# Local attention and top-2 mixture of experts on one core: attention on quarters of the array, whole loads of tile pairs, routing in phases, row writes spread over two blocks

## The chip, the core and the metric

The kernel runs on one core of one Trainium2 chip. The core has a matrix engine (TensorE, PE in the profile, with PEld for its weight loads), VectorE (DVE), ScalarE (ACT), GpSimd (POOL) and SyncE (SP), and 16 DMA engines that move data between HBM and the on-chip memory. The metric is the device time in microseconds. Before the change it is 1012.22 us, the median of three runs (1010.86 to 1013.97).

## The reference, cut to what matters

Eight batches of 576 positions and eight heads of 64 make 4608 tokens of 512 values. Attention is local: a chunk of 64 positions sees itself only. Then each token goes to the two best of eight experts by noisy logits.

```python
scores = scale * np.matmul(q_c, k_c.transpose(0, 1, 2, 4, 3))       # chunks of 64
attn = softmax(scores); out = np.matmul(attn, v_c)                    # x: 4608 x 512
noisy = x @ w_gate + np.log1p(np.exp(x @ w_noise)) * noise
top2, top2_w = the two largest of noisy, softmax over the two
for e in range(8):
    for k in range(2):
        h = np.maximum(x[mask] @ w1[e], 0.0)                          # 512 -> 1024
        out[mask] += top2_w[mask, k, None] * (h @ w2[e])              # 1024 -> 512
```

## The kernel before

The tokens are cut into 36 tiles of 128 (two chunks of 64, eight heads as four pairs). The order of work on each engine is written out by hand: each engine runs its own list in program order and waits on semaphores.

**Attention.** `attend(it)` is one turn of a software pipeline over tiles. On TensorE it holds the scores of tile it (L390), attention times values of tile it−2 (L416), the transposition of the probabilities of tile it−1 (L406), the transposition of the result x of tile it−3 (L431) and the gate product of tile it−4 (L444). VectorE takes the maximum (L394) and subtracts it (L399), and divides the result by its row sums (L420, L423, L426). ScalarE does the exponential (L402) and copies PSUM out (L408, L435). K and V of a tile lie in a ring of six buffers that are zero off the diagonal, so that one product over 128 rows handles two heads: each half of a tile is loaded by itself (L357, L362), with q (L355) that makes five loads a tile, all issued by SP.

**Routing.** After the gate, groups of tiles, (first tile, count) = (0,4), (4,8), (12,4), (16,4), (20,8), (28,8), are routed by a generator `route(g)` whose steps are spread between VectorE's steps by `step_route(n)`, with idle yields while ScalarE or TensorE work for it. It finds the two experts of each token (L484, L488), and its rank in each expert's list by a product with a triangle of ones (L507, L509), and from these the row of a slot table in HBM. `scatter` on GpSimd then writes 128 rows of x with an indirect DMA (L567) for each tile and each of the two choices; a one-element copy into `spacer` (L565) delays it until the turn has got that far.

**Experts.** Expert 0 has three blocks of rows (three, three and four tiles of 128 slots, the last of 64), computed while the last routing is still on. Block 0 and block 1 are read once the tokens below 16 and below 28 are in the slot table (`EARLY`), block 2 after all. `gather(i)` issues a block's loads on SP (L198, dynamic for later experts L203). `x_tile` transposes the gathered rows (L242 on TensorE for the first blocks, L246 on VectorE for later ones), `layer1` and `layer2` multiply in high and low halves, three products each (`three`, L259), with L278 and L281 between the layers; `weigh` (L288) scales an output by its token's weight and `store` adds it to `out` by an indirect DMA on GpSimd (L226). `out` is zeroed first by 37 writes of 256 KB (`zero_out`, L626). The other experts follow in an order that is found at run time; SP reads it from memory (L772) before it can load their weights (`w_load`, L103 and L105). `w_split` (L116, L117) cuts staged weights into halves.

SP's list after attention, then, is: 28 zero writes, block 1's gather, nine zero writes, block 2's gather, the reads of the order, expert 1's w1 (four loads of 512 KB), the gather of the following block.

Of the kernel before, what the change touches and what calls it, by code (L numbers as in the profile page):

```python
# [19 lines left out]
P = 128  # L20
# [29 lines left out]
def kernel(ctx, tc, qT, kT, vh, wgn, noise, w1, w2, out, caps=CAPS):  # L50
# [36 lines left out]
    nc.vector.memset(caprow[:, 0:1], float(caps[0]))  # L87
    run8 = consts.tile([P, NE], FT, name="run8")
# [32 lines left out]
    gate = pg.enter_context(tc.tile_pool(name="gate", bufs=1, side="right"))  # L121
# [11 lines left out]
    EARLY = {0: 2, 1: 4}  # L133
# [3 lines left out]
    groups = [(0, 4), (4, 8), (12, 4), (16, 4), (20, 8), (28, 8)]  # L137
# [14 lines left out]
    rot = {"xg": 0, "tr": 0, "l1": 0, "l2": 0}  # L152
# [131 lines left out]
    def weigh(i, j, r, p):  # L284
        e = BL[i][0]
        o = OB[0].tile([P, DM], FT, name="o")
        w = weights_of(i, j)[0:r]
        nc.vector.tensor_scalar(o[0:r], p[0:r], w, None, op0=OP.mult)  # L288
# [51 lines left out]
    vs = pv_pools.enter_context(tc.tile_pool(name="vs", bufs=1, side="right"))  # L340
    loads = pk.enter_context(tc.tile_pool(name="loads", bufs=1))
    RING = 6
    KB = [loads.tile([P, 2, 4, P], FT, name=f"kb{n}") for n in range(RING)]
    VB = [vs.tile([P, 2, 2, 4, 65], FT, name=f"vb{n}") for n in range(RING)]
    QB = {}
    HALF = (slice(0, 64), slice(64, 128))
    for n in range(RING):
        for t in (KB[n], VB[n]):
            for h in range(2):
                (nc.vector if n < 2 else nc.gpsimd).memset(t[HALF[1 - h], h], 0.0)  # L350

    def load_qk(t):
        if t < NT:
            QB[t] = loads.tile([P, 4, P], FT, name="qb", bufs=RING)
            nc.sync.dma_start(QB[t], qT[:, t])  # L355
            for h in range(2):
                nc.sync.dma_start(KB[t % RING][HALF[h], h], kT[HALF[h], t])  # L357

    def load_v(t):
        if t < NT:  # L360
            for h in range(2):
                nc.sync.dma_start(VB[t % RING][HALF[h], h], vh[HALF[h], t])  # L362

    nc.scalar.preload_act_table_set("natural_log_exp_and_others")
    for j in range(5):
        load_qk(j)
        if j:
            load_v(j - 1)
# [7 lines left out]

    PR, PT, XS, XT, RC = {}, {}, {}, {}, {}
    by_head = lambda a: a.rearrange("p (g k) -> p g k", k=64)
    sco = [by_head(PS[:, b, :]) for b in range(2)]
# [7 lines left out]
    def scores(t):  # L387
        for hp in range(4):
            for s in HALF:
                nc.tensor.matmul(PS[s, t % 2, hp * P:(hp + 1) * P], QB[t][:, hp, s], KB[t % RING][:, :, hp, s], start=True, stop=True)  # L390

    def soft_max(t):
        mx = work.tile([P, 8], FT, name="mx", bufs=2)
        nc.vector.tensor_reduce(mx, sco[t % 2], AX.X, OP.max)  # L394
        return mx

    def soft_sub(t, mx):
        PR[t] = work.tile([P, 512], FT, name="pr")
        nc.vector.tensor_tensor(by_head(PR[t]), sco[t % 2], mx[:, :, None].to_broadcast([P, 8, 64]), OP.subtract)  # L399
# [12 lines left out]
    def pv(t):  # L412
        for hp in range(4):
            for c, s in enumerate(HALF):
                o = 130 * (hp % 2)
                nc.tensor.matmul(PS[s, 3 + hp // 2, o:o + 130], PT[t][:, hp, s], VB[t % RING][:, :, c, hp, :], start=True, stop=True)  # L416

# [7 lines left out]
    def norm_c(t):  # L425
        nc.vector.tensor_tensor(x_at(t)[:, 0:DM].rearrange("p (b g k) -> p b g k", b=2, k=64), pvb[:, :, :, 0:64], RC[t].to_broadcast([P, 2, 4, 64]), OP.mult)  # L426
# [6 lines left out]
    def x_copy(t):  # L433
        XT[t] = gx.tile([P, ND, P], FT, name="xt")
        nc.scalar.activation(XT[t].rearrange("p d n -> p (d n)"), PS[:, 5, :], AF.Copy)  # L435

    def lg_at(t, n=1):
        g = grp_of[t]
        c = 256 * (g % 2) + 16 * (t - groups[g][0])
        return PS[:, 6, c:c + 16 * n]  # L440

    def gate_mm(t):
        for d in range(ND):
            nc.tensor.matmul(lg_at(t), XT[t][:, d, :], wg[:, d, 0:16], start=(d == 0), stop=(d == ND - 1))  # L444

    IDLE = 6

    def route(g):
# [9 lines left out]
        lg = lg_at(t0, G).rearrange("p (g a e) -> p g a e", a=2, e=NE)  # L458
# [3 lines left out]
        parts = [(XS[t0 // 4 + a], slice(4 * a, 4 * a + 4)) for a in range(G // 4)]  # L462
        nc.scalar.activation(y, lg[:, :, 1, :], AF.Abs)
# [4 lines left out]
        for _ in range(IDLE):  # L468
            yield

        V.scalar_tensor_tensor(u, u, -1.0, y, op0=OP.add, op1=OP.subtract)
        yield
        V.tensor_sub(sp, sp, u)
        yield
        V.scalar_tensor_tensor(sp, z[:, :, 1, :], 0.0, sp, op0=OP.max, op1=OP.add)
        yield
        V.tensor_mul(sp, sp, nz[:, t0:t0 + G, :])
        yield
        V.tensor_add(sp, sp, z[:, :, 0, :])
        yield  # L480
        m = gate.tile(n8, FT, name="gm")
        mi = gate.tile(n8, U32, name="gmi")
        for r in range(G):
            V.max(m[:, r], sp[:, r])  # L484
            if r % 2:
                yield
        for r in range(G):
            V.max_index(mi[:, r], m[:, r], sp[:, r])  # L488
            if r % 2:
                yield  # L490
        oh = gate.tile([P, 2, G, NE], FT, name="goh")
        for k in range(2):
            V.tensor_tensor(oh[:, k], be(e_row), br(mi[:, :, k]), OP.is_equal)
            yield
        for x, s in parts:
            V.scalar_tensor_tensor(x.bitcast(I32)[:, :, CODE], mi[:, s, 0], 8192.0, tok[:, ts][:, s], op0=OP.mult, op1=OP.add)
        ohb = gate.tile([P, G + 1, NE], BF, name="gohb")
        V.memset(ohb[:, G], 0.0)
        V.tensor_add(ohb[:, 0:G], oh[:, 0], oh[:, 1])
        ex, sm = nm("gex"), nm("gsm")  # L500
        V.tensor_sub(ex, m[:, :, 1], m[:, :, 0])
        yield
        nc.scalar.activation(ex, ex, AF.Exp)
        for _ in range(IDLE):
            yield
        rk = PS[:, 7, o:o + 8 * (G + 1)].rearrange("p (g e) -> p g e", e=NE)
# [3 lines left out]
        for _ in range(IDLE):  # L510
            yield
        V.tensor_scalar(sm, ex, 1.0, 1e-9, op0=OP.add, op1=OP.add)
        for i in EARLY:
            if g == EARLY[i] + 1:
                V.tensor_scalar(run8[:, 0:1], run8[:, 0:1], float(NE * P * (blocks[0][i][-1][0] + 1)), None, op0=OP.max)
        yield
        r8 = n3("gr8")
        V.scalar_tensor_tensor(r8, rk[:, 0:G], 8.0, be(run8), op0=OP.mult, op1=OP.add)
        for x, s in parts:
            V.reciprocal(x[:, :, WA], sm[:, s])  # L520
        yield
        ohr = gate.tile([P, 2, G, NE], FT, name="gohr")
        V.tensor_mul(ohr, oh, r8[:, None].to_broadcast([P, 2, G, NE]))
        V.scalar_tensor_tensor(run8, rk[:, G], 8.0, run8, op0=OP.mult, op1=OP.add)
        yield
        for i in EARLY:
            if g == EARLY[i]:
                V.tensor_copy(lim0[i], run8[:, 0:1])
        if g == LAST:

# [7 lines left out]
            yield  # L538
# [9 lines left out]
            yield  # L548
        with nc.allow_low_precision(reason="one whole number below 2**24 among zeros"):
            V.tensor_reduce(lii[:, :, ts], ohr, AX.X, OP.add)  # L550
        for x, s in parts:
            V.tensor_mul(x[:, :, WB], ex[:, s], x[:, :, WA])
        yield
# [50 lines left out]
    def step_route(n):  # L604
        for _ in range(n):
            while routing:
                try:
                    next(routing[0])
                    break
                except StopIteration:  # L610
                    routing.pop(0)

    def finish_route():
        while routing or pending:
            step_route(1)
# [12 lines left out]
    def attend(it):  # L628
        STEPS = 2
        if it > 0:  # L630
            load_qk(it + 4)
            load_v(it + 3)
# [6 lines left out]
        if it in (12, 14, 16, 18):  # L639
            w_load(0, 1, (it - 12) // 2)  # L640
        if it in (29, 31, 33, 35):
            w_load(0, 2, (it - 29) // 2)
        if it < NT:
# [7 lines left out]
        if 0 <= it - 4 < NT:  # L651
            gate_mm(it - 4)
            if grp_of[it - 4] != grp_of.get(it - 3):
                routing.append(route(grp_of[it - 4]))
        if it < NT:
            mx = soft_max(it)
            step_route(STEPS)
            soft_sub(it, mx)
            scatter(1, mx[0:1, 0:1])
            step_route(STEPS)  # L660
            soft_exp(it)
        if 0 <= it - 3 < NT:
            x_copy(it - 3)
        if 0 <= it - 2 < NT:
            norm_a(it - 2)
            step_route(STEPS)
            norm_b(it - 2)
            scatter(1, RC[it - 2][0:1, 0, 0])
            step_route(STEPS)
            norm_c(it - 2)  # L670
            step_route(STEPS)
        if it in range(20, 28):
# [26 lines left out]

    TURNS = (((1, 1), (1, 5), (2, 1)), ((0, 6), (1, 2), (1, 6), (2, 2)))  # L700
    tail = [NT + 2 + a for a in range(2)]

    def hook_tail(f, d):
# [6 lines left out]
        else:  # L710
            step_route(4)

    for i in range(NBL + 1):
# [15 lines left out]
        def hook1(f):  # L729
# [4 lines left out]
            if i == 0:  # L734
                scatter(2, HT[0][f][0][0:1, 0:1].bitcast(FT))
# [8 lines left out]
        def hook2_r(k, f):  # L744
            hook2_f(k, f)
            step_route(2)
            if f % 2 == 0:
# [12 lines left out]
        if i == 0:  # L760
            pa.close()
            block_x(1)
            OB[0] = pb.enter_context(tc.tile_pool(name="ob", bufs=4))
        if i == 0:
            zero_out(NT)
            resolve_early(0)
            layer2(0, hook2_r)
            finish_route()
            last_rows.close()
            block_h(1)  # L770
            for r in range(1, NE):
                place[r] = nc.values_load(order[0:1, r:r + 1], engines=[mybir.EngineType.SP], min_val=0, max_val=NE - 1)  # L772
            for c in range(4):
                w_load(1, 1, c)
# [138 lines left out]
```

## Time and profile before

| quantity | value |
|---|---|
| median of the runs | 1012.22 us |
| profiled execution: time | 1013.9 us |
| profiled execution: span | 1011.6 us |
| mean granted clock of TensorE | 0.989 |
| tile 0's scores, tile 35's scores | 5.5 us, 151.6 us |
| layer 1 and layer 2 of expert 0, block 0, begin | 164.8 us, 189.0 us |
| TensorE busy | 971.4 us (96%) |
| VectorE, ScalarE, GpSimd busy | 453.9 us, 275.8 us, 227.5 us |

The profile shows one execution. A row of the timeline is: start, duration, engine, line, operation, output and inputs by the program's names, the sizes, the number of instructions, and in brackets the idle time in front of it with what ended it. "SPq" is an instruction by which SP issues a DMA.

### The profile page before, as it was taken

The page shows a single profiled execution, that of the slowest core. Times are in us where ns is not written, and L with a number is a line of the kernel's source. Part 1 is how long each engine was busy: PE and PEld are TensorE (multiplying, and loading weights), DVE is VectorE, ACT ScalarE, POOL GpSimd, SP SyncE. Part 2 cuts the span into 40 slices and gives each one's busy share as a digit, 9 for nine tenths or more (in the row PEclk, how much of TensorE's full clock was granted, in tenths as well). Part 3 has the DMA queues.
Part 4 walks back from the last instruction along what each step waited for, and adds up shares of the span by engine and source line. Part 5 has one row for each costly group of instructions (what it writes and reads, how often), then busy time and mean ns, then how long its engine had stood idle before and what let it go on. Part 6 is the DMA issues. An engine that isn't in the chain of part 4 may idle for free. (4 is left out here: it accounts for less than half of the span.)

```text
span 1011.6 us, 16090 instructions
## 1 busy us (share of the span) xinstructions
PE 971.4 (96%) x5930; PEld 874.3 (86%) x5930; DVE 453.9 (45%) x1015; ACT 275.8 (27%) x574; POOL 227.5 (22%) x332
## 2 busy tenths in 40 slices
PE   6999898999799999999999999999999999999996
PEld 5888887898689799989998999899989998999885
DVE  6667665522435354355434542454245334533311
ACT  2444543211314132213211421232123222322200
POOL 3034754751020201110111011101110111101112
PEclk9999999999799999999999999999999999999998
DMA  8899999865470335233622372246235423512213
GB/s 230 260 299 308 339 315 396 308 180 128 81 188 14 64 115 153 32 53 105 172 32 45 112 179 32 42 114 170 32 70 148 105 32 84 167 21 32 32 19 45
DMA packets 103217, 132.92 MB, mean 131 GB/s; under 512 B 22848, under 2 KB 56000, under 8 KB 103136
## 3 DMA queue, kind: packets, MB, share of 16 engines
q1 hardware_dynamic: 86704, 93.54, 30.4%
q0 software_dynamic: 16432, 38.33, 19.2%
q8 instruction: 47, 0.77, 0.3%
q14 instruction: 34, 0.28, 0.1%
HBM read 81.69 MB, written 50.13 MB: 130 GB/s over the span
## 5 line engine op out<-in xcount | busy, mean ns | idle before, releaser
L259 PE MATMUL PS<-xh,w1h 128*128 128x384 f32 (+2 forms) x768 | 262.8, 342 | 9.0 <-DVE hl L281 7.3
L226 POOL DMA_INDIRECT out<-o,lid x77 | 119.3, 1549 | 672.8 <-DVE o L288 645.0
L259 PE MATMUL PS<-xl,w1h 128*128 128x384 f32 (+2 forms) x768 | 261.7, 341 | 0.0
L259 PE MATMUL PS<-xh,w1l 128*128 128x384 f32 (+2 forms) x768 | 261.6, 341 | 0.0
L259 PE MATMUL PS<-w2h,hh 128*128 128x512 f32 x584 | 227.9, 390 | 0.0
L259 PE MATMUL PS<-w2h,hl 128*128 128x512 f32 x584 | 227.7, 390 | 0.0
L259 PE MATMUL PS<-w2l,hh 128*128 128x512 f32 x584 | 227.6, 390 | 0.0
L278 ACT ACTIVATE hh<-PS 128x384 fp32r<-128x384 f32 (+2 forms) x192 | 95.0, 496 | 445.9 <-PE PS L259 440.7
L281 DVE SCALAR_TENSOR_TENSOR hl<-PS,hh 128x384 fp32r<-128x384 f32 (+2 forms) x192 | 108.5, 566 | 178.8 <-ACT hh L278 140.0
L259 PEld LDWEIGHTS PS<-xh,w1h 128*128 128x128 f32 x768 | 145.4, 189 | 15.1 <-DVE hl L281 7.7
L288 DVE TENSOR_SCALAR o<-PS,lwt 128x512 f32<-128x512 f32 x77 | 57.4, 749 | 218.3 <-PE PS L259 207.0
L259 PEld LDWEIGHTS PS<-xl,w1h 128*128 128x128 f32 x768 | 145.3, 189 | 1.7
L259 PEld LDWEIGHTS PS<-xh,w1l 128*128 128x128 f32 x768 | 145.3, 189 | 1.1
L259 PEld LDWEIGHTS PS<-w2h,hl 128*128 128x128 f32 x584 | 109.2, 187 | 23.5
L259 PEld LDWEIGHTS PS<-w2l,hh 128*128 128x128 f32 x584 | 109.2, 187 | 22.5
L259 PEld LDWEIGHTS PS<-w2h,hh 128*128 128x128 f32 x584 | 109.2, 187 | 22.5
L567 POOL DMA_INDIRECT slots<-xs,lii x72 | 72.6, 1009 | 22.3 <-issue 19.9
L249 ACT ACTIVATE xh<-y 128x512 fp32r<-128x512 f32 x67 | 41.2, 614 | 106.3 <-DVE y L246 100.2
L250 DVE TENSOR_TENSOR xl<-y,xh 128x512 fp32r<-128x512 f32 x67 | 44.9, 671 | 48.2 <-ACT xh L249 44.7
L246 DVE STREAM_TRANSPOSE y<-xg 128x512 f32<-128x512 f32 x67 | 45.6, 681 | 13.1 <-DMA xg<-slots 13.1
L416 PE MATMUL PS<-vb,pts 128*64 128x130 f32 x576 | 40.4, 279 | 10.5 <-ACT xt L435 3.6
L390 PE MATMUL PS<-kb,qb 128*64 128x128 f32 x576 | 41.2, 288 | 9.5 <-DMA kb<-in_kT 9.5
(118 smaller groups left out, 712.3 us busy)
## 6 DMA issues: line engine op xcount, KB each, us to landing
st<-in_w SPq DMA_DIRECT2D x64, 512.0 KB
xg<-slots SPq DMA_DIRECT2D x252, 64.0 KB
out<-zero SPq DMA_DIRECT2D x37, 256.0 KB
vb<-in_vh SPq DMA_DIRECT2D x72, 130.0 KB
qb<-in_qT SPq DMA_DIRECT2D x36, 256.0 KB
kb<-in_kT SPq DMA_DIRECT2D x72, 128.0 KB
xg<-slots SPq DMA_DIRECT2D x9, 256.0 KB
slots<-zero SPq DMA_DIRECT2D x8, 257.5 KB
```

The source lines that it names most:

```text
L226: s = nc.gpsimd.indirect_dma_start(out=out, out_offset=bass.IndirectOffsetOnAxis(ap=rows_of(i, j)[0:r], axis=0), in_=o[0:r], in_offset=Non ...
L246: nc.vector.transpose(y[:, 0:4 * r], x[:, 0:4 * r])
L249: nc.scalar.activation(oh, src, AF.Copy)
L250: nc.vector.tensor_sub(ol, src, oh.bitcast(FT))
L259: nc.tensor.matmul(p, a, b, start=first and n == 0, stop=last and n == 2)
L278: nc.scalar.activation(hh[:, 0:n], p, AF.Relu)
L281: nc.vector.scalar_tensor_tensor(hl[:, 0:n], p, 0.0, hh[:, 0:n].bitcast(FT), op0=OP.max, op1=OP.subtract)
L288: nc.vector.tensor_scalar(o[0:r], p[0:r], w, None, op0=OP.mult)
L390: nc.tensor.matmul(PS[s, t % 2, hp * P:(hp + 1) * P], QB[t][:, hp, s], KB[t % RING][:, :, hp, s], start=True, stop=True)
L416: nc.tensor.matmul(PS[s, 3 + hp // 2, o:o + 130], PT[t][:, hp, s], VB[t % RING][:, :, c, hp, :], start=True, stop=True)
L567: s = nc.gpsimd.indirect_dma_start(out=slots, out_offset=bass.IndirectOffsetOnAxis(ap=lii[:, k, t0 + r:t0 + r + 1], axis=0), in_=XS[(t0 + ...
```

## The change

- **Attention on quarters.** Scores and values use 64x64 quarters of the array: sixteen instructions of 64x64 (scores) and 64x65 (values) a tile in place of eight of twice the width, each over the 64 rows of one head. K and V need no zeros, so the ring and its memsets go. The scores have one pair of PSUM banks for all tiles, where before two tiles alternated.
- **Whole loads.** Each of q, k and v is loaded for a pair of tiles at once (512, 512 and 520 KB, with 4 KB a partition), three loads per pair, five pairs deep.
- **Gate.** One product for four tiles with the gate weights as the stationary side, on four column groups, then a copy and a small product with `sel` that adds the groups (`gate_sum`).
- **Routing.** Seven groups. The generator yields the names of phases ("act", "wait", "dve", "pe"); each engine gets its phase last in its turn, at most six VectorE steps a turn.
- **Expert 0.** w1 is loaded at turns 9 to 15 (before 12 to 18) and its low half made on GpSimd in every second turn from 12 to 26. Three turns of attention, not two, lie inside the first layer 1. The scatters that are left go two per step of layer 1 of blocks 0 and 1, and one at every third step of layer 2. `finish_route` follows layer 1 of block 1. `next_weights` (the order reads and expert 1's w1) is called inside layer 2 of block 0 once the routing is empty; what stood behind it (the following block's buffers, its gather and the table of rows) moves behind layer 1 of block 1. Outputs get two buffers, and two more from block 1 on, in place of four.

```diff
-    groups = [(0, 4), (4, 8), (12, 4), (16, 4), (20, 8), (28, 8)]
+    groups = [(0, 4), (4, 4), (8, 4), (12, 4), (16, 4), (20, 8), (28, 8)]
...
-            for s in HALF:
-                nc.tensor.matmul(PS[s, t % 2, hp * P:(hp + 1) * P], QB[t][:, hp, s], KB[t % RING][:, :, hp, s], start=True, stop=True)
+            for h, c in HC:
+                r, s = slice(h * 64, h * 64 + 64), slice(c * 64, c * 64 + 64)
+                o = 64 * hp
+                nc.tensor.matmul(PS[s, h, o:o + 64], q[r, t % 2, hp, s], k[r, t % 2, hp, s], start=True, stop=True)
...
+            for h, c in HC:
+                r, s = slice(h * 64, h * 64 + 64), slice(c * 64, c * 64 + 64)
+                nc.tensor.matmul(PS[s, 3 + h, hp * 65:hp * 65 + 65], PT[t][r, hp, s], v[r, t % 2, c, hp, :],
+                                 start=True, stop=True)
...
+    def gate_mm(g):
+        for d in range(ND):
+            nc.tensor.matmul(PS[32 * d:32 * d + 32, 6, :], wg[:, d, :], XT[g][:, d], start=True, stop=True)
...
+    def gate_sum(g):
+        for r in range(4):
+            nc.tensor.matmul(lg_at(4 * g + r), LS[g][:, r, :], sel, start=True, stop=True)
...
+        if it % 2 == 0 and it >= 2 and it // 2 + 3 < NT // 2:
+            load_q(it // 2 + 3)
+            load_k(it // 2 + 3)
...
+        step_route("dve", STEPS)
+        if it in range(12, 28, 2):
             w_split(0, 1, *wq.pop(0), eng=nc.gpsimd)
...
+    def next_weights():
+        for r in range(1, NE):
+            place[r] = nc.values_load(order[0:1, r:r + 1], engines=[mybir.EngineType.SP], min_val=0, max_val=NE - 1)
+        for c in range(4):
+            w_load(1, 1, c)
...
-            if i == 0:
-                scatter(2, HT[0][f][0][0:1, 0:1].bitcast(FT))
+            if i <= 1:
+                scatter(2, HT[i][f][0][0:1, 0:1].bitcast(FT))
...
+            if i == 0 and not place and (0, 3) <= (k, f) and not routing:
+                next_weights()
+            if f % 3 == 0:
                 scatter(1)
...
+        elif i == 1:
             finish_route()
+            if not place:
+                next_weights()
```

How the change moves instructions shows best on two engines. On TensorE, a turn of attention before (kb and qb are K and Q, vb V, pts the transposed probabilities, xt the transposed x, wg the gate weights):

```order
L390 MATMUL PS<-kb_140,qb 64x128 x8
L416 MATMUL PS<-vb_144,pts 64x130 x8
L406 MATMUL PS<-ident,pr 128x128 x4
L431 MATMUL PS<-ident,xs 128x128 x4
L444 MATMUL PS<-wg,xt 128x16 x4
```

and the turn with a gate product, and the next with its sum, now:

```order
L395 MATMUL PS<-kb,qp 64x64 x16
L422 MATMUL PS<-vb,pts 64x65 x16
L411 MATMUL PS<-ident,pr 128x128 x4
L438 MATMUL PS<-ident,xs 128x128 x4
L450 MATMUL PS<-xt,wg 32x512 x4
L395 MATMUL PS<-kb,qp 64x64 x16
L422 MATMUL PS<-vb,pts 64x65 x16
L411 MATMUL PS<-ident,pr 128x128 x4
L438 MATMUL PS<-ident,xs 128x128 x4
L463 MATMUL PS<-sel,ls 128x16 x4
```

The order of the steps within a turn is the same; the gate's part stands once in four turns, each time over two neighbouring turns.

On SP, behind the last loads of attention, before (xg are gathered rows, the first three of block 1, the last four of block 2; the order reads follow):

```order
L105 DMA st<-in_w 128x2x512 x2
L626 DMA out<-zero 128x512 x28
L198 DMA xg<-slots 128x512 x3
L582 DMA meta_118<-slots 128x3x3
L626 DMA out<-zero 128x512 x9
L198 DMA xg<-slots 128x512 x3
L198 DMA xg<-slots 64x512
L772 TENSOR_LOAD order
L772 ISA x2
```

and now, first from block 0's gather to the first of the seven order reads, then from the last two of expert 1's four w1 loads to the gathers of blocks 1 and 2:

```order
L202 DMA xg<-slots 128x512 x3
L600 DMA meta_121<-slots 128x3x3
L109 DMA st<-in_w 128x2x512 x2
L655 DMA out<-zero 128x512 x37
L738 TENSOR_LOAD order
L738 ISA x2
```

```order
L107 DMA st<-in_w 128x1x1024
L107 ISA
L107 DMA st<-in_w 128x1x1024
L202 DMA xg<-slots 128x512 x3
L600 DMA meta_122<-slots 128x3x3
L202 DMA xg<-slots 128x512 x3
```

The zero writes are now one run of 37; the reads of the order and expert 1's w1 loads stand in front of the gathers of blocks 1 and 2, where they stood behind them. The first transposition of block 1 keeps its place in TensorE's list: in the middle of layer 2 of block 0, at step (1,1).

More of the change, by code (lines that the diff above doesn't have):

```diff
@@ L528, in route @@
                 V.tensor_copy(lim0[i], run8[:, 0:1])
+        for x, s in parts:
+            yield "dve"
+            V.tensor_mul(x[:, :, WB], ex[:, s], x[:, :, WA])
+        yield "dve"
+        with nc.allow_low_precision(reason="one whole number below 2**24 among zeros"):
+            V.tensor_reduce(lii[:, :, ts], ohr, AX.X, OP.add)
         if g == LAST:
+            yield "dve"
             key = gate.tile([P, NE], FT, name="gkey")
@@ L547, in route @@
             V.tensor_reduce(cape, by_e, AX.X, OP.add)
[L548 to L553, printed above, removed]
         pending.extend((g, r, k) for r in range(G) for k in range(2))
@@ L602, with step_route, next_turn, route_turn @@
     routing = []
[L604 to L611, printed above, removed]
+    def step_route(phase, most=99):
+        for r in list(routing):
+            while r[1] == phase and most > 0:
+                if phase == "dve":
+                    most -= 1
+                r[1] = next(r[0], None)
+            if r[1] is None:
+                routing.remove(r)
+    def next_turn():
+        for r in routing:
+            if r[1] == "wait":
+                r[1] = next(r[0])
+    def route_turn(n):
+        next_turn()
+        step_route("pe")
+        step_route("act")
+        step_route("dve", n)
     def finish_route():
         while routing or pending:
-            step_route(1)
+            route_turn(4)
             scatter(1)
@@ L650, in attend @@
             x_trans(it - 3)
[L651 to L654, printed above, removed]
+        gated = it - 4 >= 0 and (it - 4) % 4 == 3
+        if gated:
+            gate_mm((it - 4) // 4)
+        step_route("pe")
+        if it - 5 >= 0 and (it - 5) % 4 == 3:
+            gate_sum((it - 5) // 4)
+            if grp_of[it - 5] != grp_of.get(it - 4):
+                r = route(grp_of[it - 5])
+                routing.append([r, next(r)])
         if it < NT:
             mx = soft_max(it)
-            step_route(STEPS)
             soft_sub(it, mx)
-            scatter(1, mx[0:1, 0:1])
-            step_route(STEPS)
+            scatter(1, mx[0:1, 0, 0:1])
             soft_exp(it)
@@ L697 @@
         x_tile(0, k)
+    def next_weights():
[3 more added lines that the diff above has]
+            w_load(1, 1, c)
     TURNS = (((1, 1), (1, 5), (2, 1)), ((0, 6), (1, 2), (1, 6), (2, 2)))
[L701 removed]
+    tail = [NT + 2 + a for a in range(3)]
     def hook_tail(f, d):
```

187 lines of the change are left out of this document (92 added, 95 removed).

## The prediction

> **What bounds the kernel now.** I read the page's span first, then a table of stretches, then the turn of attention on TensorE and on VectorE, and last SP's queue between the stages.
>
> ```profile
> span 1011.6 us, 16090 instructions
> ...
> 24.00:151.60 127.60, 116.63 (x1459) 107.15 (x1455) 84.75 (x327) 58.58 (x127) 55.27 (x86) 0.99 0.97 304
> 151.60:164.80 13.20, 10.77 (x121) 9.55 (x120) 7.71 (x22) 5.74 (x11) 6.40 (x11) 1.00 1.05 386
> ...
> 257.00:270.00 13.00, 5.87 (x18) 5.30 (x19) 6.47 (x11) 4.17 (x8) 0.00 (x0) 0.61 0.44 64
> 270.00:1012.00 742.00, 733.26 (x3696) 658.54 (x3694) 307.56 (x509) 181.24 (x377) 112.62 (x141) 1.00 0.37 83
> ```
>
> In each stretch stand its length, the busy time of PE, PEld, DVE, ACT and POOL, the granted clock, the DMA share and GB/s. From 270 us on TensorE works 733 of 742 us at full clock, and the change edits nothing there, so only the first 270 us can move. They fall into attention (tile 35's scores start at 151.6, which I call s35), expert 0, and one hole at 257 to 270 us. In attention two things are near their limit at once: TensorE (116.6 of 127.6 us) and the DMA engines (0.97 of their time).
>
> ```profile
> 5.50 2.92 PE L390 MATMUL PS<-kb,qb 128*64 128x128 f32 x23 [5.50 <-DMA kb<-in_kT]
> ...
> 81.34 1.09 PE L390 MATMUL PS<-kb,qb 128*64 128x128 f32 x16
> 82.26 1.06 PE L416 MATMUL PS<-vb,pts 128*64 128x130 f32 x16
> 83.25 0.65 PE L406 MATMUL PS<-ident,pr 128*128 128x128 f32 x4
> 83.74 0.60 PE L431 MATMUL PS<-ident,xs 128*128 128x128 f32 x4
> 84.18 0.96 PE L444 MATMUL PS<-wg,xt 128*128 128x16 f32 x8
> 85.07 0.33 PE L390 MATMUL PS<-kb,qb 128*64 128x128 f32 x2
> ...
> 154.11 0.69 DVE L394 TENSOR_REDUCE mx<-PS 128x8 f32<-128x512 f32 x1 [1.12 <-PE PS L390]
> 154.84 0.69 DVE L399 TENSOR_TENSOR pr<-PS,mx 128x512 f32<-128x512 f32 x1
> 155.44 0.16 DVE L420 TENSOR_SCALAR rc<-PS 128x8 f32<-128x8 f32 x1
> 155.63 0.20 DVE L423 RECIPROCAL rc<-rc 128x8 f32<-128x8 f32 x1
> 155.87 0.69 DVE L426 TENSOR_TENSOR xs<-PS,rc 128x512 f32<-128x512 f32 x1
> ```
>
> A turn of one tile on TensorE without a wait is 85.07 − 81.34 = 3.73 us: scores 0.92, values 0.99, two transposes 0.49 and 0.44, gate 0.89. (151.6 − 5.5) / 35 gives 4.17 us a tile as run, so about 0.45 us of a turn is waiting. On VectorE the five instructions of a turn take 154.11 to 156.56, 2.4 us.
>
> **Attention: what the turn becomes.** Sixteen score instructions of 128 moving columns start within 0.92 us, two at a time on the two column halves, one pair each 0.115 us. The changed kernel has thirty-two of 64 columns. No row of this profile shows two instructions side by side on different row halves. If four run at once they take eight steps of half that, 0.46 us; if only two, 0.92 us, as now; if one, 1.84. Values go the same way, 0.50, 1.0 or 2.0. I take four at once: the quarters share neither rows nor columns, which is the same independence as that of the column halves that do overlap. The gate's eight instructions a tile (0.89 us) become eight wide ones per four tiles plus eight small sums per four tiles; 512 columns at 0.115 for 128 are 0.46, and four column groups at once make two steps of eight instructions, 0.92, with 0.89 for the sums: 1.81 / 4 = 0.45 us a tile. The turn is 0.46 + 0.50 + 0.49 + 0.44 + 0.45 = **2.3 us** (3.3 with two at once, 5.2 with one).
>
> So TensorE drops below VectorE, whose five instructions stay 2.4 us and which also routes.
>
> ```profile
> L488 DVE FIND_INDEX8 gmi<-gm,gsp 128x8 uint32<-128x8 f32 x28 | 4.1, 162 | 0.0
> ...
> L515 DVE TENSOR_SCALAR run<-run 128x1 f32<-128x1 f32 x1 | 0.1, 148 | 0.0
> ...
> 120.02 1.28 POOL L117 TENSOR_TENSOR w1l<-st,w1h 128x512 fp32r<-128x512 f32 x1
> 121.23 0.18 POOL L565 COPY spacer<-mx 1x1 f32<-1x1 f32 x1
> ...
> 122.59 0.18 POOL L565 COPY spacer<-rc 1x1 f32<-1x1 f32 x1
> ```
>
> The 22 routing lines of VectorE in 24 to 151.6, from the largest to the smallest of these two, add to 26 us for the 28 tiles routed there, 0.94 us a tile; with seven groups in place of six I take **1.0**, bounds 0.8 (now partly beside other work) and 1.25 (the fixed instructions of each group of four). The turn is then 3.4 us once routing runs, and 2.45 us for the first nine tiles. GpSimd comes close behind: a scatter with its spacer copy takes 1.36 us (121.23 to 122.59), two of them 2.7, and half a weight split 0.64, 3.4 us in turns 15 to 26. The removed memsets of the ring and the single score buffer cost nothing: scores of the next tile only need the subtraction, the second of the five, and the last three and the routing cover the 0.46 us. Costs of this kind are at most that 0.46 a tile if the cover were gone, 16 us, which would still not be a loss against now.
>
> s35 = 6.5 (first load in place of 5.5: 512 KB and not 256 ahead of it) + 9 × 2.45 + 26 × 3.4 = 117; with 0.25 us of waiting a tile, half of today's, **125**. Lower bound 117. Upper bound by DMA:
>
> ```profile
> vb<-in_vh SPq DMA_DIRECT2D x72, 130.0 KB
> qb<-in_qT SPq DMA_DIRECT2D x36, 256.0 KB
> kb<-in_kT SPq DMA_DIRECT2D x72, 128.0 KB
> ...
> slots<-zero SPq DMA_DIRECT2D x8, 257.5 KB
> ```
>
> 28 MB of loads, 2 of routing zeros, 2 of w1 (four of 512 KB) and 40 scatters of 0.26 MB (128 rows with their codes), 42 to 43 MB, must move before s35. At the 304 GB/s of the row at share 0.97 that is 138 us, and 143 with the slow start; at the 386 of the row behind it, 109. 125 asks for 340, which lies between these rows and nearest their middle. Before, five issues a tile on SP are now three per two tiles, so SP no longer paces the start.
>
> The Trainium skill (DMA: Bandwidth & Descriptors, "iDMA fabric") tabulates a load stream of 4 KiB rows, which the loads now have, at 408.7 GB/s. By that the DMA engines would not bind and s35 would be 117; the row with 304 GB/s at share 0.97 says that mixed traffic here does not reach it.
>
> **What the gain runs into.** SP's queue decides when block 1's rows come.
>
> ```profile
> 151.53 28.62 SPq L626 DMA_DIRECT2D out<-zero  x28
> 191.12 1.34 SPq L198 DMA_DIRECT2D xg<-slots  x3
> 192.51 0.43 SPq L582 DMA_DIRECT2D meta<-slots  x1
> 192.99 9.72 SPq L626 DMA_DIRECT2D out<-zero  x9
> 224.28 1.92 SPq L198 DMA_DIRECT2D xg<-slots  x4
> 230.97 6.02 SPq L103 DMA_DIRECT2D st<-in_w  x4
> 237.79 26.95 SPq L203 DMA_DIRECT2D xg<-slots  x16
> ...
> 232.00:260.00 28.00, 24.82 (x122) 21.39 (x120) 4.47 (x7) 2.67 (x5) 4.21 (x6) 0.98 0.49 119
> ...
> 195.15 0.60 PE L242 MATMUL PS<-ident,xg 128*128 128x128 f32 x4
> ...
> 261.44 0.71 DVE L246 STREAM_TRANSPOSE y<-xg 128x512 f32<-128x512 f32 x1 [13.05 <-DMA xg<-slots]
> 264.13 0.74 PE L259 MATMUL PS<-xh,w1h 128*128 128x448 f32 x1 [7.31 <-DVE hl L281]
> ...
> 268.78 0.53 PE L259 MATMUL PS<-xh,w1h 128*128 128x448 f32 x1
> 269.14 0.37 PE L259 MATMUL PS<-xl,w1h 128*128 128x448 f32 x1
> ```
>
> Expert 1's four w1 loads are issued at 230.97, and the rows gathered behind them are first used at 261.44: 30.5 us for 2.1 MB and a few gathers, while the table shows 119 GB/s in that stretch. Their source walks an outer dimension of four. That load is the cause of the hole: VectorE waits 13.05 us for the rows, TensorE 7.31 us, and its instructions of 448 columns then start 0.37 to 0.38 us apart until 268.8, twice what they do later (0.21): 5 us at half speed, 2.5 lost. The whole hole costs 9.8.
>
> In the changed kernel these four loads stand ahead of block 1's three gathers, behind all 37 zero writes and the reads of the experts' order. The chain: the last scatter of group 3 ends on GpSimd in turn 32, which VectorE finishes a turn behind, at s35 − 10.2 + 3.4 + 1.7 = s35 − 5.1, and lands about 1.5 later; gather of block 0, its meta and two w2 loads take 3.0 (1.34 + 0.43, and an estimate of as much as the gather for the two loads); 37 zeros take 28.62 + 9.72 = 38.3; the order reads 4.8 (226.2, where the gathers' 1.92 end, to 230.97); w1 and the gather 29.5 (30.5 less a part for the sixteen gathers). Block 1's rows land at s35 − 3.6 + 3.0 + 38.3 + 4.8 + 29.5 = **s35 + 72**.
>
> TensorE comes there sooner. Before, layer 1 of expert 0 begins at 164.8 (s35 + 13.2) and the first transposition of block 1 stands at 195.15, 30.3 later; the change brings s35 + 11.3 (one tail turn more lies inside layer 1) + 30.3 = s35 + 42. The transposition sits in TensorE's stream in front of the rest of layer 2, so TensorE **stops for 30 us** (26 to 35 by the bounds of its terms), at a place where it did not wait at all before. The stall brings about 2.5 us at half clock, as the hole did. What is behind SP's gather waits with it: gathers of block 2 and of the later experts, whose first use is some 45 us on, so they are in time, and the hole at 264 goes.
>
> The Trainium skill (DMA: Bandwidth & Descriptors, "Why a DMA increments its semaphore by 16 and not by 1") says that a transfer uses the largest number of engines up to 16 that divides both slowest dimensions; with four rows outermost that is four. A quarter of its 408.7 GB/s would make the loads 21 us and the stall 22; 119 GB/s with other traffic in it agrees with four engines, and the 30.5 us measured here stand in the sum.
>
> The scatters moved to two blocks are work of GpSimd beside TensorE; they hold up block 1's gather only if they end later than s35 + 42, and the last of group 5 is issued by layer 2 at step (0,3), s35 + 38, so they do not. Later scatters, and the end of the route behind layer 1 of block 1, lie beside that layer's work on TensorE; block 2's gather needs them only 30 us later.
>
> **The sum.** Rest from block 1's transposition, before: 1011.6 − 195.15 = 816.4; less the hole with its clock, 9.8, plus 2.5 for the new one: 809. Two output buffers for block 0 in place of four I cost at nothing: an output waits for the store two before it, and a store on GpSimd takes 1.5 us, less than TensorE's 24 instructions for one output.
>
> ```profile
> L226 POOL DMA_INDIRECT out<-o,lid x77 | 119.3, 1549 | 672.8 <-DVE o L288 645.0
> ```
>
> Span = s35 + 72 + 809 = 1006 at 125, against 1011.6 before. The profiled run is 1013.9, 2.3 above its span, so 1008.3 for it; the median shown is 1.7 lower than the profiled run, so **1006.6**, rounded to 1007.
>
> **Rivals.**
> - Slower: DMA paces attention. If the mixed rate stays at the 304 of the row, s35 is 138 to 143 and the time 1020 to 1025, as everything behind hangs on s35. It decides from s35 = 133 on (1015). For it: share 0.97. Against it: 386 and the larger rows. 0.2.
> - Block 1's gather does not wait for the w1 loads, or these are quicker beside less traffic: the stall is 5 to 12 us, 982 to 990. For it: nothing in the rows; against it: 261.44. 0.1.
> - The quarters of one column half do not overlap: the turn is 3.3 on TensorE, still below 3.4, and nothing changes except less slack: s35 at 130, 1012. 0.15. If they run one by one, 5.2 us a turn, 1070; 0.03.
> - No waits in attention: s35 at 117, 999. 0.15.
> - The forecast: the change does what it says and the sum holds, 1002 to 1011. 0.37.
>
> **The numbers.** A measurement of this kernel can tell 0.3%, 3 us, from no change; that puts the borders at 1009.2 and 1015.2. Faster: five sixths of the forecast (0.31) and the two quick cases (0.25), 0.56. Within: the rest of the forecast and the turn with half the overlap, 0.21. Slower: DMA and the serial quarters, 0.23. With a tenth left out at each end the range is 988 to 1021; the likeliest case alone is 1002 to 1011.
>
> **What will show it.** Right: turns of about 3.4 us with VectorE nearly full and TensorE's share near 0.7 in attention; scores of a tile in about half a microsecond; a gap of some 30 us on TensorE ahead of block 1's transposition, released by the gather, with the w1 loads ahead of it at about 80 GB/s; no hole at the old place. Wrong: DMA at share 1.0 and turns near 4 us; a gather that lands before TensorE needs it; TensorE's turn above 3.4.

## The result

| | before | changed |
|---|---|---|
| time, median of six runs | 1012.49 us (1010.86 to 1013.97) | 1019.66 us (1018.39 to 1023.23) |
| ratio | | 1.0079, 95% interval 1.006 to 1.0098 |
| span of the profiled run | 1011.6 us | 1017.6 us |
| tile 35's scores (s35) | 151.6 us | 132.2 us |
| layer 1 of expert 0 begins | 164.8 us | 143.0 us |
| TensorE's stop ahead of block 1's transposition | none | 39.5 us |
| hole ahead of the other experts' first rows | 7.3 us | none |
| TensorE busy | 971.4 us | 938.1 us |

The kernel became 0.8% slower. Attention ends 19 us sooner and TensorE has 33 us less to do, but the time in which it does nothing grows from 40.2 to 79.5 us, by as much as one stop of 39.5 us ahead of block 1's transposition. The stretches of the changed kernel (length, busy time of PE, PEld, DVE, ACT and POOL, granted clock, DMA share, GB/s):

```profile
6.00:24.00 18.00, 13.47 (x348) 11.17 (x348) 12.06 (x24) 6.96 (x13) 0.00 (x0) 1.00 1.03 410
24.00:51.00 27.00, 20.57 (x526) 16.50 (x527) 17.94 (x57) 12.65 (x27) 0.00 (x0) 0.91 1.04 394
51.00:132.00 81.00, 69.10 (x1705) 58.37 (x1703) 65.71 (x245) 48.92 (x110) 50.04 (x77) 0.90 0.83 294
171.00:210.00 39.00, 0.06 (x1) 0.00 (x0) 0.00 (x0) 0.00 (x0) 9.37 (x18) 0.56 0.57 181
270.00:1017.00 747.00, 739.28 (x3726) 664.17 (x3724) 310.96 (x514) 183.83 (x382) 112.88 (x141) 1.00 0.37 81
```

DMA moved 394 to 410 GB/s at the start and then had room (share 0.83), and behind its first load TensorE waits for no load in attention, so DMA doesn't pace it any more. Between 171 and 210 TensorE, VectorE and ScalarE do nothing. SP's queue says why, and TensorE's row says what it waited for:

```profile
131.41 1.38 SPq L202 DMA_DIRECT2D xg<-slots  x3
...
133.37 0.99 SPq L109 DMA_DIRECT2D st<-in_w  x2
134.41 39.21 SPq L655 DMA_DIRECT2D out<-zero  x37
181.21 6.71 SPq L107 DMA_DIRECT2D st<-in_w  x4
188.03 7.96 SPq L202 DMA_DIRECT2D xg<-slots  x3
...
210.52 1.12 PE L246 MATMUL PS<-ident,xg 128*128 128x128 f32 x4 [39.46 <-DMA xg<-slots]
```

Block 1's gather is issued at 188 and used at 210.5. Ahead of it stand 39 us of zero writes, 7.6 us of order reads (173.6 to 181.2) and expert 1's w1.

TensorE's timeline in attention: the first scores, the second tile's, a run of values with a stop in it, a turn without a stop of any kind, and the scores of tile 35:

```profile
6.02 1.14 PE L395 MATMUL PS<-kb,qp 64*64 64x64 f32 x32 [6.02 <-DMA kb<-in_kT]
8.69 1.13 PE L395 MATMUL PS<-kb,qp 64*64 64x64 f32 x32 [1.53 <-DVE pr L404]
...
35.90 0.50 PE L395 MATMUL PS<-kb,qp 64*64 64x64 f32 x17
...
47.26 0.41 PE L422 MATMUL PS<-vb,pts 64*64 64x65 f32 x14
49.91 0.81 PE L422 MATMUL PS<-vb,pts 64*64 64x65 f32 x18 [2.24 <-issue]
...
104.86 0.69 PE L395 MATMUL PS<-kb,qp 64*64 64x64 f32 x32
105.38 0.66 PE L422 MATMUL PS<-vb,pts 64*64 64x65 f32 x32
105.97 0.66 PE L411 MATMUL PS<-ident,pr 128*128 128x128 f32 x4
106.46 0.60 PE L438 MATMUL PS<-ident,xs 128*128 128x128 f32 x4
106.99 1.07 PE L450 MATMUL PS<-xt,wg 128*32 128x512 f32 x8
107.99 0.69 PE L395 MATMUL PS<-kb,qp 64*64 64x64 f32 x32
...
132.21 0.69 PE L395 MATMUL PS<-kb,qp 64*64 64x64 f32 x32 [1.00 <-DVE pr L404]
```

TensorE's waits over the attention stage (what it waited for, us in all, times, the longest):

```profile
PE PS L422 <- issue: 10.7, 9, 2.9
PE PS L395 <- DVE pr L404: 4.9, 7, 1.5
PE PS L395 <- DVE rc L430: 1.7, 1, 1.7
...
PE PS L395 <- issue: 1.6, 2, 0.9
```

Scores take 0.52 us and values 0.59, where they took 0.92 and 0.99 before. But TensorE stops inside a run of these instructions with nothing to wait for (the rows at 47.26 and 49.91 are the two parts of one run of 32). The largest group of its waits is of that kind; three of its nine, of 0.39 us each, stand ahead of a run. Before it was 1.6 us in all. The second group, 4.9 us, is new too: the scores have one pair of banks now, so a tile's scores wait until VectorE has subtracted in the tile before. The wait at 8.69 is the first of these.

Held against the DMA records, each of the nine stops inside a run ends a nearly fixed time after a transfer of 16 KB on the queue for instructions begins:

```
a stop inside scores or values ends at   18.5  30.6  37.1  49.9  69.5  80.7  92.8  99.7  117.0 us
from one start to the next              1.15  0.89  0.88  2.46  0.85  1.74  0.23  3.10   1.79 us
the 16 KB began ahead of that by         2.35  2.41  2.42  2.49  2.39  2.46  2.45  2.39   2.39 us
```

From 8 to 132 us (packets, MB, share of the 16 engines) that queue had 11 packets before:

```profile
8.00:132.00 124.00, 112.14 (x1398) 102.12 (x1396) 80.12 (x281) 55.81 (x118) 48.19 (x74) 0.99 0.96 296
...
q8 instruction: 11, 0.18, 0.6%
```

and in the changed kernel 20:

```profile
8.00:132.00 124.00, 102.01 (x2545) 85.07 (x2545) 94.96 (x323) 68.53 (x149) 50.04 (x77) 0.92 0.90 330
...
q8 instruction: 20, 0.33, 1.1%
```

That is one packet for some 254 of TensorE's instructions (products and weight loads together, 2794 and 5090) in both kernels, so the packets are TensorE's instructions.

### The profile page after: what moved, and what is told of

It reads as the page before. It is cut to its first block, busy times and chain, and to the rows that moved or that the text cites. A ratio compares the mean times of both kernels' runs of the same rounds, so it can differ in the third digit from the quotient of the medians.

```text
span 1017.6 us, 17885 instructions
## 1 busy us (share of the span) xinstructions
PE 938.1 (92%) x6939; PEld 834.0 (82%) x6939; DVE 454.3 (45%) x1025; ACT 281.6 (28%) x589; POOL 218.8 (22%) x316
## 4 chain that ended last, share of the span: by engine, by line
PE 84%; DMA 5%; DVE 4%; issue 3%; SPq 3%; POOL 1%; ACT 0%; DVEq 0%; POOLq 0%; ACTq 0%
PE PS L263 76%; DMA xg<-slots 2%; PE PS L395 2%; SPq L655 2%; PE PS L422 1%; DMA out<-zero 1%; DVE mx L399 1%; PE PS L411 1%; PE PS L308 1%; DMA st<-in_w 1%; PE PS L438 1%; DVE pr L404 1%; SPq L738 1%; SPq L107 1%; DVE xs L433 1%
## 5 line engine op out<-in xcount | busy, mean ns | idle before, releaser
L229 POOL MEMSET spacer<- 1x1 f32 x77 | 45.3, 589 | 0.0
L395 PEld LDWEIGHTS PS<-kb,qp 64*64 64x64 f32 x1152 | 23.9, 154 | 25.5 <-issue 8.3
```

The costliest lines, as they stand in the source:

```text
L229: nc.gpsimd.memset(spacer, 0.0)
L395: nc.tensor.matmul(PS[s, h, o:o + 64], q[r, t % 2, hp, s], k[r, t % 2, hp, s], start=True, stop=True)
```

## The experiments

They ran on other occasions than the two kernels above: e1 to e4 on one chip, the others on a second one, in two groups (a0 and e5 to e7; e8 and e10 to e12). Some expectations speak of the second chip; whether it was the chip or the moment isn't known. The kernel before took 1015.4, 1016.5 and 1014.3 us there (medians in this order), and each ratio is to that of its own group. The changed kernel ran in a0's group alone, 1031.57 us, so differences of the others from it carry an uncertainty of 1 to 2 us. e5, e6, e7 and e10 ran once each (1058, 1029, 1061 and 1023 us), and only their attention is read.

**The changed kernel again (a0).**

> The changed kernel as it is, again. In its first profile tile 35's scores started at 132.2 us; in the profiles of e1, e2 and e3, which edit nothing ahead of that place, at about 148, with some 25 us of short stops inside the score and value instructions of TensorE that end on nothing the profile shows (10 stops, 14.9 us, in the first profile). If the place in memory of the edited kernels' code makes these stops, this run shows 132 and few stops, 1018 to 1022 us. If they belong to the chip or the moment, it shows stops like e1's, 145 to 150 for tile 35 and about 1030 to 1036 us.

1031.57 us, ratio 1.0161 (1.0132 to 1.0191). Tile 35's scores came at 146.3. So the later attention of e1, e2 and e3 (tile 35 at 148.3 to 148.5) is not of their making. Up to 65 us the stops are those of the first profile; from there on there are two short ones in most turns, of which only a few end 2.4 us after a transfer of instructions began:

```profile
120.46 0.45 PE L422 MATMUL PS<-vb,pts 64*64 64x65 f32 x8
121.34 0.30 PE L422 MATMUL PS<-vb,pts 64*64 64x65 f32 x3 [0.44 <-issue]
122.08 0.59 PE L422 MATMUL PS<-vb,pts 64*64 64x65 f32 x21 [0.43 <-issue]
...
120.65 0.99 POOL L585 DMA_INDIRECT slots<-xs,lii  x1 [0.16 <-issue]
```

The stop for block 1 was 35.3 us here: attention is later, and GpSimd's scatters with it, but the chain on SP has the same terms, and block 1's rows were used 76.7 us after tile 35's scores began.

**The w1 loads behind the gathers (e1).**

```diff
-            if i == 0 and not place and (0, 3) <= (k, f) and not routing:
-                next_weights()
```

> The order reads and expert 1's w1 loads behind the gathers of blocks 1 and 2, everything else as changed. Theory A (the 39.5 us stop of TensorE is the w1 loads and order reads ahead of block 1's gather): the gather is issued right behind the zero writes, at about 174 us, and lands near 176; TensorE stops 5 to 8 us instead of 39.5. A hole of 5 to 15 us comes back later, where the first rows of the other experts queue behind the same loads. Time 985 to 998 us. Rival B (the gather waits for the scatters of the routing or for the zero writes' traffic, the w1 loads only happen to be in front): the stop stays above 25 us, time above 1005.

1016.26 us, ratio 1.0004 (0.9988 to 1.002); against the changed kernel's 1031.57 that is some 15 us. SP's queue, one of GpSimd's scatters and TensorE's two gaps:

```profile
146.87 38.18 SPq L655 DMA_DIRECT2D out<-zero  x37
196.34 1.30 SPq L202 DMA_DIRECT2D xg<-slots  x3
...
228.69 1.95 SPq L202 DMA_DIRECT2D xg<-slots  x4
235.38 6.42 SPq L107 DMA_DIRECT2D st<-in_w  x4
...
193.37 0.97 POOL L585 DMA_INDIRECT slots<-xs,lii  x1 [0.22 <-issue]
...
199.24 1.11 PE L246 MATMUL PS<-ident,xg 128*128 128x128 f32 x4 [9.41 <-DMA xg<-slots]
...
267.46 0.74 PE L263 MATMUL PS<-xh,w1h 128*128 128x448 f32 x1 [5.96 <-DVE hl L285]
```

The stop falls from 35.3 to 9.4 us, and the old hole is back with 6.0, as theory A has it. The stop is a little above theory A's 5 to 8 us, and the time is far above its range, for two reasons: attention was 16 us later than in the first profile, and the gather did not follow the zero writes, which end at 185. The rows that it reads are complete with the last scatter of group 5, the 56th of all, which GpSimd ends at 194.3 (the row at 193.37); the gather is issued 2.0 us later. That second limit stands behind the first one. In the first profile the 56th scatter ends at 175.0, so there the gather could have been issued some 11 us before the 188.0 at which it was.

**w1 by loads of 32 partitions (e2), and both edits (e3).**

```diff
-            nc.sync.dma_start(st, w1v[ds(place[e], 1), c].rearrange("o j r f -> (o j) r f") if e else ...)
+            if e:
+                for j in range(4):
+                    nc.sync.dma_start(st[32 * j:32 * j + 32], w1v[ds(place[e], 1), c, j].rearrange("o r f -> (o r) f"))
```

> Each w1 load of the experts 1 to 7 as four loads of 32 partitions, whose source has 32 rows outermost and not four; order as changed. Theory A with the loads slow because four of 16 engines carry them: sixteen issues at 0.5 to 0.55 us, about 9 us, so block 1's gather lands at 192 to 196 us in place of 210; the stop is 21 to 25 us, time 1001 to 1006. If the loads are slow for another reason (the state of memory behind the zero writes, the reads by run-time address): 210 us or later and 1019 to 1025.

> Both edits. Theory A: stop of 5 to 8 us at block 1's gather and no hole for the other experts' first rows, 978 to 988 us. If only the order counts: the same as e1. If the later hole is set by the last scatters and not by the loads: the same as e1.

e2: 1019.68 us, ratio 1.0036 (1.0021 to 1.0051). e3: 1008.36 us, ratio 0.9919 (0.9894 to 0.9945). In e2:

```profile
196.74 8.35 SPq L109 DMA_DIRECT2D st<-in_w  x16
205.20 1.61 SPq L206 DMA_DIRECT2D xg<-slots  x3
...
209.75 1.11 PE L250 MATMUL PS<-ident,xg 128*128 128x128 f32 x4 [19.85 <-DMA xg<-slots]
...
198.00:208.00 10.00, 0.00 (x0) 0.00 (x0) 0.00 (x0) 0.00 (x0) 4.82 (x8) 0.50 0.95 303
```

and a stretch of the changed kernel's first profile in which only w1 is under way:

```profile
203.00:207.00 4.00, 0.00 (x0) 0.00 (x0) 0.00 (x0) 0.00 (x0) 0.00 (x0) 0.50 0.25 104
```

From the first w1 issue to the use of the gathered rows it is now 13.0 us; in the changed kernel it was 29.3 (181.21 to 210.52). The same bytes from the same place to the same place came more than twice as fast when the source had 32 rows outermost in place of four. The two stretches show why: with four rows outermost the DMA share is 0.25, four of 16 engines, at 104 GB/s (the records of w1's 4 KB packets have 4.1 of them under way at a time on average), and with 32 rows 0.95 and 303 GB/s, the gathers and scatters included. All four loads had been issued by 188 us, so it isn't that too few of them were in flight.

The stop is 19.9 us, just below the range of theory A. But the rows' 209.75 us and the time are what the other expectation had (210 or later, 1019 to 1025), and theory A's 192 to 196 us and 1001 to 1006 are missed. Both were reckoned from the first profile; here tile 35 came 16 us later, and the order reads, which began at 184.6, ended at 196.7, 12 us later (7.6 in the first profile); why they took so long isn't known. In e3 the stop is 9.4 us as in e1 and there is no later hole, as theory A has it; the time is 20 us above its range for the two reasons named at e1.

**The same loads in the kernel before (e4).** The edit of e2, on the kernel before.

> The kernel before, with its w1 loads of experts 1 to 7 split into loads of 32 partitions. Theory A: the hole at 257 to 270 us goes, since expert 1's w1 arrives in about 9 us in place of 28; 9.8 us less, 1001 to 1005 us. If the hole has another cause: 1010 to 1015.

1005.69 us, ratio 0.9887 (0.9849 to 0.9924), 9.7 us of medians, where 9.8 were expected. The hole is gone; in the two stretches in which it stood TensorE works throughout, at full clock:

```profile
232.00:260.00 28.00, 28.00 (x139) 24.36 (x138) 10.13 (x16) 6.06 (x11) 4.84 (x6) 1.00 0.79 147
257.00:270.00 13.00, 13.00 (x63) 11.51 (x63) 7.59 (x21) 6.75 (x13) 0.00 (x0) 1.00 0.53 82
```

**Half as many instructions (e7), twice the score instructions (e5).** e7 has 8 products of 64 rows by 128 columns; both chunks use the first one's keys. e5 issues each score twice.

> Scores and values with 8 instructions of 64 rows and 128 columns in place of 16 of 64x64: both chunks of a tile use the first chunk's keys and values. TensorE's time for the steps should stay, the number of its instructions for scores and values halves. Theory I (TensorE's stops inside these steps come from its instructions running out, 64 starts in half a microsecond, fetched 16 KB at a time): the stops nearly go, below 4 us in all, and tile 35's scores come at 118 to 124 us. Rival (the stops come from the width of the quarters or from PSUM shared with the other engines): they stay, 10 us or more.

> Each score instruction issued twice, the second writing the same values. Theory I: a half more instructions per turn, so the stops inside scores and values grow to 1.5 to 2 times those of the changed kernel on the same chip, and tile 35's scores come 10 to 25 us later. Rival (the stops come from something else, TensorE has room): VectorE stays the bound, the stops stay, tile 35 moves by less than 4 us.

e7: the stops inside scores and values are gone but for one at 9.4 us. Tile 35's scores came at 175.4 and not at 120, for a reason outside both theories:

```profile
79.43 1.11 PE L395 MATMUL PS<-kb,qp 64*128 64x64 f32 x16
80.38 1.06 PE L422 MATMUL PS<-vb,pts 64*128 64x65 f32 x16
...
82.39 1.11 PE L395 MATMUL PS<-kb,qp 64*128 64x64 f32 x16
```

Sixteen records of 64 rows and 128 columns take 0.95 us, 0.059 each, one behind the other: row halves of full width did not run side by side here, quarters do, four at once (32 in 0.52). Besides, in most turns every instruction took twice as long (5.5 us a turn where the one from 79.43 to 82.39 has 2.96). From 96.5 to 130.7 us the granted clock was 0.50; from 24 to 65 us it reads 1.00 and the turns were as slow, which is not explained. As TensorE was slow, it also fetched less often, so e7 alone doesn't settle theory I.

To compare the stops I count starts more than 0.2 us apart inside a run, from 8 us to tile 35's scores; that makes 10 and 14.9 us in the first profile (the wait at 8.69 is among them) and 33 and 25.2 us in a0. e5: tile 35 came at 173.0, 26.7 us later, just past theory I's range, and the stops grew to 44 and 39.1 us, 1.55 times, within the 1.5 to 2 that it asked; the long ones, above 1.4 us, went from three to nine. The rival's 4 us is out by far. But 32 scores more a tile, at 0.5 us, are 18 of the 26.7 us by themselves, so the delay alone shows only that TensorE has no room. The table of stops and fetches above carries theory I more than these two do.

**Without the loads (e6).**

> The loads of q, k and v are left out from the sixth pair of tiles on; the data of the first five are used again. If DMA traffic makes attention slow (late data, or fetches of instructions that stand behind the loads): the stops go and tile 35's scores come at 115 to 122 us. Theory I with a fetch limited by itself: the stops stay within a third of those of the changed kernel, and tile 35 moves by less than 5 us.

33 stops, 21.3 us in all (a0: 33 and 25.2), tile 35's scores at 143.1, 3.2 us sooner, at a DMA share of 0.34. So neither the data nor the loads' traffic on the DMA engines makes most of the stops.

**Without GpSimd's scatters (e10).**

> The rows of x go to the slot table by plain writes from SP, 128 rows after another, and not by GpSimd's indirect writes; the routing's places are left out, and the results are written to other rows, so only attention is read. On the second chip the changed kernel stopped twice a turn for 0.6 to 0.7 us from 65 us on, which is where GpSimd's scatters begin, and each pair ended 0.7 and 1.4 us after the start of the scatter behind the row sums. If the scatters make these stops: they go, what is left are the stops that end 2.4 us after a fetch of 16 KB of instructions begins (8 to 15 us in all), and tile 35's scores come 8 to 14 us sooner than 146. If not: 20 us of stops or more, as before.

Stops of 15.5 us, 13 of them, where a0 has 25.2 and 33. The pairs are gone: but for the wait at 8.5 us, each of the 12 that are left ends 2.29 to 2.60 us after a transfer of instructions begins. e8, which ran in the same group with the scatters, has the pairs (32 stops, 25.0 us), so it isn't the moment. Tile 35's scores came at 126.8, 19.5 us sooner, more than expected. The stretch of attention in a0:

```profile
24.00:146.00 122.00, 100.02 (x2229) 81.00 (x2229) 83.89 (x300) 60.54 (x136) 49.96 (x77) 0.89 0.81 287
```

and in e10:

```profile
24.00:126.00 102.00, 83.02 (x2229) 68.10 (x2228) 83.70 (x299) 60.70 (x136) 15.89 (x42) 0.98 1.00 364
```

TensorE's waits for nothing the profile shows, at the values and at the scores, in a0,

```profile
PE PS L422 <- issue: 15.3, 29, 2.4
PE PS L395 <- issue: 3.0, 5, 0.9
```

and in e10:

```profile
PE PS L420 <- issue: 6.9, 9, 2.4
PE PS L393 <- issue: 5.2, 6, 1.8
```

The granted clock rises from 0.89 to 0.98 along with it. So on that occasion the scatters cost attention some 20 us, of which the stops are 10; that the slower clock and what waits for GpSimd are the rest isn't shown. In the first profile the pairs of short stops are absent at the same scatters; why is open.

**Quarters alone (e11, e12).** The kernel before with scores and values on quarters and nothing else; e12 has e2's loads too.

> The kernel before with scores and values on quarters alone (and the score banks that go with them): ring, loads by halves, gate, routing and the order behind attention stay. If the quarters bring the gain in attention: TensorE's turn without a wait falls below 3 us, tile 35's scores come at 138 to 148 us (before 151.6 on the first chip), and as nothing stops TensorE for block 1 most of it is left at the end, 1003 to 1012 us where the kernel before takes 1015 to 1016. If whole loads, gate and routing brought it: tile 35 within 2 us of before, or later by the stops of instructions, 1013 to 1022.

> e11 and w1 of experts 1 to 7 by loads of 32 partitions as in e4. e4 gained 9.7 us. If the two edits add: 993 to 1003 us. If an earlier start of the experts only makes TensorE wait for block 1's rows, whose scatters go no faster on GpSimd: 1001 to 1006, no better than e4.

e11: 1029.57 us, ratio 1.0142 (1.0096 to 1.0188); tile 35 at 166.3. e12: 1017.39 us, ratio 1.0027 (0.9999 to 1.0055). Both miss.

```profile
24.00:151.00 127.00, 109.31 (x2144) 102.60 (x2146) 73.16 (x270) 51.59 (x113) 48.73 (x74) 0.79 0.93 282
```

With half loads DMA stays near 282 GB/s, and the granted clock is 0.79: TensorE has less to do and does it slower. Alone, the quarters cost 15 us. The gain in attention is that of quarters together with whole loads, the gate for four tiles and the routing in phases; which of these carries it was not tried.

**Later transpositions (e8).** e3 with

```diff
-    TURNS = (((1, 1), (1, 5), (2, 1)), ((0, 6), (1, 2), (1, 6), (2, 2)))
+    TURNS = (((2, 2), (2, 4), (2, 6)), ((0, 6), (1, 2), (1, 6), (2, 2)))
```

> e3, and the transpositions of block 1 at the end of layer 2 of block 0, steps (2,2), (2,4), (2,6) in place of (1,1), (1,5), (2,1), some 6 us of TensorE's work later. In e3 the gather waited for the last scatter of group 5 on GpSimd and not for SP, and TensorE stopped 9.4 us. Theory A: the stop falls to 2 to 5 us, the time by 4 to 8 us from e3's 1008.4, to 1000 to 1005 us on a chip on which the kernel before takes 1015 to 1016. Rival (the wait moves to where layer 1 of block 1 needs the transposed rows): no gain, 1006 to 1010.

1005.14 us, ratio 0.9902 (0.9868 to 0.9937), about 3 us below e3 by the medians and 4.6 by the spans (1007.1 to 1002.5). As the kernel before differs by 1.1 us between the two groups and the intervals of the ratios overlap, a gain over e3 isn't shown. The transposition no longer waits; what is left is one gap of 1.9 us ahead of it (at 197.3, behind VectorE's output). e8 and e4 beat both kernels, and their intervals overlap. e8 still has the stops of attention in it: tile 35's scores came at 148.1, where the first profile of the changed kernel has 132.2.

## Why the prediction was wrong

It said 1007 with faster as the likeliest, and the kernel is slower. The time lies in the stated range, 988 to 1021; the sign is wrong. The two large terms are there and of their kind: attention becomes shorter, and TensorE stops for block 1's rows behind the w1 loads. The steps that failed are two terms of the sum, s35 = 125 (132.2 measured) and the 72 us of the chain behind it (78.3), both too small. The gain in attention is 19.4 us and not 26.6, and the stop 39.5 and not 30.

- **Quarters, four at once:** right. 0.52 and 0.59 us for scores and values against 0.46 and 0.50; 64 rows by 128 columns would not have done it (e7).
- **VectorE bounds the turn, s35 = 125:** this step failed. With its waiting of 0.25 us a tile the sum has 24.3 us for the first nine tiles and 94.9 for the other 26 (with 6.5 for the first load 125.7, written as 125); they took 29.9 (6.0 to 35.9) and 96.3 (35.9 to 132.2). Most of what is missing lies in the first nine. There TensorE waited 2.0 us for VectorE's subtraction, 1.6 for ScalarE's exponential and 1.6 for instructions, and its first turns ran at half speed (scores 0.91 us, though the clock row reads 1.00). The single score buffer was put at nothing; over the whole stage its waits are 4.9 us.
- **That the other 26 came near 3.4 and 0.25 is luck.** From 36 to 132 us VectorE worked 76.8 of 96 us, 2.96 a turn and not 3.4, and TensorE 79.0, 3.04 a turn; neither is nearly full. What the turn of 3.70 has beyond that is waiting, 0.7 and not 0.25. The largest part of TensorE's are its stops for instructions, 10.7 us here. Behind the three that end at 49.9, 99.7 and 117.0 the granted clock was 0.50 (50 to 59.5, 101 to 104 and 118 to 121), though in e10 stops as long were not followed by that. The step counted the time of twice as many instructions half as long, and not their number.
- **DMA as the rival that decides the sign:** wrong. The whole loads moved 394 to 410 GB/s. The sentence with 408.7 GB/s from the Trainium skill (DMA: Bandwidth & Descriptors, "iDMA fabric") was right for the start of this kernel (410 and 394 GB/s), and the row with 304, from loads of half the size a row, was the wrong one to extend.
- **The chain on SP:** the mechanism was right and its size 6.3 us short. Rows landed at s35 + 78.3 (210.5 − 132.2), not 72. Block 0's gather was issued 2.8 us later against s35 than reckoned (131.4, s35 − 0.8, in place of − 3.6): the last scatter of group 3 ended at 127.7, s35 − 4.5 for − 5.1, and the gather came 3.7 us behind it and not 1.5; the zero writes took 39.2 for 38.3; the order reads 7.6 for 4.8, five of the seven at 0.8 to 1.1 us while DMA still moved 338 GB/s (174 to 180), where before most took 0.27; w1 and gather 29.3 for 29.5.
- **TensorE's arrival:** 171.1, s35 + 38.8, 3.2 sooner than s35 + 42. With the chain's 6.3 that makes the stop 39.5 and not 30.
- **The rest:** 1017.6 − 210.5 = 807.1 against 809: right, and the hole went as said. Sum of the errors on the span: 7.2 + 6.3 − 2 = 11.5, and 1006 + 11.5 = 1017.5. Either large term alone would have left the kernel near its old time.
- **The w1 loads are slow since four engines carry them:** borne out by e2 and e4, and by the DMA share of 0.25 in the first profile. Their order ahead of the gather is worth some 15 us (e1), their speed some 12 (e2), and both 23 (e3), by the medians against a0; behind both stands the last scatter of group 5.

## What to carry to other kernels

A stage that becomes faster is worth only what the next stage can take: list what the transfers behind it wait for, in queue order, and put a load that nothing needs soon behind the ones that the next instruction of the bound engine needs. Look at the outermost dimension of a slow load; splitting one into four took a 30 us load to 13 here and gained 1% in a kernel that was otherwise left alone. When an edit doubles the number of instructions and halves their size, count the instructions as a resource beside their time.

## What the runs showed of the hardware

- TensorE's instructions arrive in transfers of 16 KB, one for some 254 of them. Where TensorE stopped inside a run with nothing to wait for, it resumed 2.35 to 2.49 us after such a transfer began (nine stops of nine in the first profile; 2.29 to 2.60 us and 12 of 12 in e10).
- Row halves of 64 by 128 ran one after the other in e7 (0.059 us each), quarters of 64 by 64 four at once (32 in 0.52 us).
- GpSimd's indirect writes can stop TensorE's issue: pairs of stops, mostly of 0.6 to 0.7 us, on one occasion, none on the other with the same kernel, and none when the writes were left out there (e10). How they do it is open.
- A load of 128 partitions whose source has four blocks outermost is slow: from the issue of four such loads (2.1 MB) to the use of what is queued behind them 29.3 us, and 13.0 with each as four loads of 32 rows. While nothing else moved, it kept the DMA engines at a share of 0.25, 104 GB/s. The Trainium skill (DMA: Bandwidth & Descriptors, "Why a DMA increments its semaphore by 16 and not by 1") gives the rule: the largest number of engines up to 16 that divides both outermost dimensions. e2 and e4 agree with it.
- The granted clock and the stops don't go together in a simple way. It was 0.99 in the attention of the kernel before, 0.91 in the first profile with nine stops, 0.89 in a0 with 32, 0.98 in e10 with 12 and 0.79 in e11 (24 to 151 us); what sets it is open.
